# Seven quarter products for the second layer of the leading expert's first two blocks, with their gates made beside the last attention chunks and the row squares cleared by ScalarE

## The chip, the cores and the metric

The kernel runs on one core of one Trainium2 chip. The metric is the device time of one launch in microseconds; the median of three runs of the kernel before is 391.99 us (391.74 to 392.34).

## What is computed

A gated linear attention over 4 x 768 tokens and 8 heads of 48 dimensions gives rows of 384 features. Each of the 3,072 rows then goes to one of 8 experts by its cosine similarity, and the expert's two-layer network is scaled by the routing probability. Cut to what matters:

```python
state = alpha[:, :, t, :, None] * state + np.einsum('bhd,bhe->bhde', k[:, :, t], v[:, :, t])
y[:, :, t] = np.einsum('bhd,bhde->bhe', q[:, :, t], state)
...
logits = xn @ en.T / tau                      # xn, en: rows over their norms
expert_idx = np.argmax(logits, axis=1)
probs = np.exp(logits - logits.max(-1, keepdims=True)); probs /= probs.sum(-1, keepdims=True) + 1e-09
gate_w = probs[np.arange(N), expert_idx]
h = np.maximum(x[mask] @ w1[e], 0.0)          # 384 -> 1024
out[mask] = gate_w[mask, None] * (h @ w2[e])  # 1024 -> 384
```

## The kernel before

**The attention part** takes the tokens in 24 chunks of 128 rows. The loop over `s` is a software pipeline: in step `s` TensorE turns chunk `s`, VectorE runs two scans over it (`r` in `decays`, `a` in `decay_queries`), GpSimd multiplies the queries with `a` (`qs`), TensorE makes the scores of chunk `s - 1` (`sc`, masked by VectorE into `sm`), mixes chunk `s - 2` (`mix_states`, `mix_chunk`) and makes the output rows and router logits of chunk `s - 3` (`rows`). VectorE chooses experts by groups of chunks (`choose`, `place`), and GpSimd scatters each chunk's rows with their logits and token number to the DRAM buffer `xs`, sorted by expert (`to_rows`).

**The leading expert.** After 16 chunks some expert is sure to have 256 rows. It is found on VectorE (`first_expert`), and once chunk 15 is scattered, `fetch_early` has SyncE load its first two blocks of 128 rows into `exg` (the tile `xg_s[2]`). TensorE turns them (`turn_early`) and does their first layer in eight pieces beside the last three steps (`first_layer_early`, relu by ScalarE into `ehT`). After the last chunk VectorE counts the rows of each expert (`counts`, which ends with `pads` and `used_i`). GpSimd scatters blank rows behind each expert's rows (eight scatters of `blank` to `pads`) and clears the two tiles `xq` (two memsets); SyncE fetches the blocks of the experts in turn.

**The expert part** runs the experts in the order of turns, the leading one as number 0. Before `run(0)` come the gates of the two early blocks (`gates`: maximum, differences, row squares and root, exponential, sum, reciprocal, on VectorE and ScalarE) and their second layer, plain: `second_layer` multiplies eight tiles of 384 columns a block. Between the two blocks TensorE turns the rest of expert 0 (`prepare`), and VectorE forms the 16 sums of quarter weights for run 1's first layer (`mix_first_weights(1)`, 256 columns each). `run(0)` does the remaining block of expert 0 in the plain way, while TensorE turns run 1's four blocks through two PSUM tiles (`pxg`, `ps_x`) that VectorE copies out (`turn`, L919). Runs 1 to 7 use Strassen-like forms: 28 half-width products for the first layer of three blocks (`first_layer_blocks`) and seven quarter products for the second layer of two blocks (`second_layer_pair`). Those need four weight sums `w2_m` (`mix_weights`: 768 columns each, by VectorE for run 1, by GpSimd for the others) and four sums `hT_m` of the hidden rows (`mix_hidden`).

**What sets the order.** Each engine works through its own queue in a fixed order. The Tile scheduler sets that order by priorities and its own estimate of time; `tc.issue_after(x)` (`in_turn`, `behind`, `turn_of`, `by_dve`, `by_act`) keeps an instruction behind `x`. Waits between engines are semaphores at single instructions. In VectorE's queue the loads of the early rows are not waited for before the gates; on TensorE `turn_early` waits for them.

Of the kernel before, what the change touches and what calls it, by code (L numbers as in the profile page):

```python
# [29 lines left out]
def kernel(  # L30
# [16 lines left out]
    P = 128  # L47
# [63 lines left out]
    ehT = consts.tile([P, FT, EARLY * P], FP32)  # L111
    NXG = 3
# [113 lines left out]
    with ExitStack() as c1:  # L226
# [79 lines left out]
        def prepare_logits():  # L306

            nc.vector.reciprocal(rtau, rtau)
            e2 = work.tile([E, DM], FP32, name="e2", bufs=1)
            en = work.tile([E, 1], FP32, name="en", bufs=1)  # L310
            nc.scalar.activation(e2, emb, AF.Square, accum_out=en)
# [35 lines left out]
        def choose(g):  # L347
# [18 lines left out]
            for s in range(s0, s1):  # L366
                eng = nc.vector if {S0 - 1, NS - 1, NS - 2} & set(range(s0, s1)) else nc.gpsimd
                eng.tensor_tensor(before[:, s + 1], before[:, s], chosen[:, s], ALU.add)
# [52 lines left out]
        def counts(n):  # L421
# [20 lines left out]
            nc.vector.scalar_tensor_tensor(  # L442
# [12 lines left out]
            return nc.vector.tensor_copy(used_i, used[0:1])  # L455
# [180 lines left out]
        def mix_chunk(s):  # L636
# [4 lines left out]
            for hh in range(2):  # L641
# [7 lines left out]
                nc.scalar.copy(yT[hh].rearrange("p q t -> p (q t)"), pyx[hh][:, 0:YX])  # L649
# [46 lines left out]
        def first_layer_early(f0, f1):  # L696
            for f in range(f0, f1):
# [6 lines left out]
                nc.scalar.activation(ehT[:, f], ph, AF.Relu)  # L704


# [35 lines left out]
        for s in range(NS + 3):  # L742
# [33 lines left out]
            if NS <= s < NS + 2:  # L776
                with in_turn():
                    first_layer_early(2 * (s - NS), 2 * (s - NS) + 1)
# [16 lines left out]
            if NS <= s < NS + 2:  # L795
                with in_turn():
                    rows(s - 2)
# [31 lines left out]
            if s == NS:  # L829
                with tc.issue_after(st[NS - 1]["masked"].ins):  # L830
                    nc.gpsimd.memset(w1_s[1][:, 0, 0:1], 0.0)
                weights(1)
            for r in rows_of(s):
                g = group_of[r]
                if r == GROUPS[g][1] - 1:
                    with tc.issue_after(st[min(s, NS) - 1]["dve"].ins):
                        choose(g)
                    with behind(s) if s < NS else ExitStack():
                        nc.gpsimd.tensor_copy(x_g[g][:, :, TK], toks[:, slice(*GROUPS[g])])
            if s > NS:  # L840
                with in_turn():
                    first_layer_early(2 * (s - NS) + 2, 2 * (s - NS) + 4)
        with tc.issue_after(st[NS - 1]["dve"].ins):
            routed = [counts(n)]


    with ExitStack() as c3:
        qp = c3.enter_context(tc.tile_pool(name="qp", bufs=1, reuse_waits="tile"))
        xq_s.extend(qp.tile([P, NROW // SQ, DA], FP32, name=f"xq{i}") for i in range(NXQ))
# [10 lines left out]
        yp = c3.enter_context(tc.tile_pool(name="yp", bufs=3, reuse_waits="tile"))  # L860
# [8 lines left out]
        w2_m = wp.tile([P, 4, FT // 2, DM // 2], FP32, name="w2_m")  # L869
        hT_m = xp.tile([P, 4, FT // 2, P], FP32, name="hT_m")  # L870

# [6 lines left out]


# [344 lines left out]
        def second_layer_pair(w2_t, hT, gate, col):  # L1224
# [6 lines left out]
            a, b, d = (bank(j)[:, 0:m] for j in (0, 1, 3))  # L1231
# [28 lines left out]
            gated(y1[:, m:DM], a, g1, u[:, 2])  # L1260
            product(d, s4, b22, False, True)
# [3 lines left out]
            done_pair[:] = pe[0], by_act(nc.scalar.mul, y1[:, 0:m], a, g1)  # L1265
# [34 lines left out]
        def run(i):  # L1300
# [132 lines left out]
        egt = xp.tile([P, EARLY], FP32, name="egt")  # L1433
        esx = xp.tile([P, EARLY], I32, name="esx")
        known = gates(exg[:, 0:EARLY], egt[:, 0:EARLY], esx[:, 0:EARLY], EARLY)
# [9 lines left out]
        with turn_of([known]):  # L1445
# [38 lines left out]
```

## Time and profile before

| | us |
|---|---|
| median of three runs | 391.99 (391.74 to 392.34) |
| the profiled execution | 391.01 |
| its span, first to last instruction | 389.3 |
| TensorE busy in it | 379.9 |
| VectorE busy | 283.9 |
| GpSimd busy | 261.7 |
| ScalarE busy | 194.3 |

The profile is of one execution. A row of the timeline gives start, duration, engine, line, operation, written tile and read tiles, shape and count; in square brackets stand the idle time before it and what ended it. `PE` is TensorE, `DVE` VectorE, `ACT` ScalarE, `POOL` GpSimd, `SPq` the queue of SyncE. A matmul of this type has two records. Several instructions of one kind in a row are one row, whose duration runs from the first start to the last end; in a stream the next row starts before that end.

### The profile page before, as it was taken

How to read it: one execution, taken by the hardware profiler on the slowest of the kernel's cores; microseconds unless marked ns; L12 is line 12 of the kernel's file. 1: busy time of each engine (PE TensorE's matmuls, PEld its weight loads, DVE VectorE, ACT ScalarE, POOL GpSimd, SP SyncE). 2: the span in 40 equal slices, each digit the busy share in tenths (PEclk: the TensorE clock that was granted, in tenths of full speed). 3: DMA queues.
4: the chain of work that ended last, by engine and by line, in shares of the span. 5: the costliest groups of instructions: out<-in, count | busy, mean ns of one | idle time of the engine just before them, and what ended most of it. 6: DMA issues, size and time to landing. Idle time of an engine off the chain costs nothing. (4 is left out here: it accounts for less than half of the span.)

```text
span 389.3 us, 12413 instructions
## 1 busy us (share of the span) xinstructions
PE 379.9 (98%) x4596; PEld 338.3 (87%) x4596; DVE 283.9 (73%) x687; ACT 194.3 (50%) x492; POOL 261.7 (67%) x342
## 2 busy tenths in 40 slices
PE   6999999999999999999999999999999999999994
PEld 5889899999999877779989889789979979979974
DVE  7898989889999637992973984963874596795630
ACT  3555565554556544573653734823651492472620
POOL 5365577788776548744829959929957997977201
PEclk9999999999999999999999999999999999999999
DMA  9999999999999996794947768245604810100101
GB/s 138 162 166 166 156 182 197 190 182 198 187 218 174 285 370 231 214 355 97 356 109 285 212 197 287 46 154 182 180 19 175 296 28 18 43 2 17 40 19 46
DMA packets 131181, 64.05 MB, mean 165 GB/s; under 512 B 113319, under 2 KB 127920, under 8 KB 130344
## 3 DMA queue, kind: packets, MB, share of 16 engines
q1 hardware_dynamic: 127008, 52.92, 58.2%
q0 software_dynamic: 3728, 10.16, 7.3%
q8 instruction: 43, 0.70, 0.8%
q14 instruction: 26, 0.21, 0.2%
q10 hardware_dynamic: 376, 0.05, 0.1%
HBM read 53.85 MB, written 11.45 MB: 168 GB/s over the span
## 5 line engine op out<-in xcount | busy, mean ns | idle before, releaser
L1035 DVE TENSOR_TENSOR hT<-hT,pq 128x384 f32<-128x384 f32 x84 | 44.0, 549 | 35.9 <-PE pq L1143 28.4
L889 POOL DMA_INDIRECT out_dram<-y,sx x25 | 29.7, 1188 | 54.3 <-ACTq L1381 20.3
L538 POOL TENSOR_TENSOR qs<-qc,a 128x512 f32<-128x512 f32 x24 | 30.8, 1283 | 30.0 <-DVE a L534 20.8
L1143 PE MATMUL pq<-xT_m,w_m 128*128 128x192 f32 x252 | 44.4, 326 | 0.0
L1017 PE MATMUL pyo<-w,hT 128*128 128x384 f32 x128 | 42.6, 486 | 0.0
L1143 PEld LDWEIGHTS pq<-xT_m,w_m 128*128 128x128 f32 x252 | 41.4, 190 | 0.2
L1017 PEld LDWEIGHTS pyo<-w,hT 128*128 128x128 f32 x128 | 24.1, 190 | 14.8
L1040 ACT ACTIVATE hT<-hT 128x384 f32<-128x384 f32 x56 | 26.3, 515 | 15.2 <-DVE hT L1035 14.6
L1097 POOL TENSOR_TENSOR w_m<-w,w_m 128x256 f32<-128x256 f32 x42 | 31.1, 753 | 2.0 <-PE pq L1143 0.6
L1055 POOL TENSOR_TENSOR w_m<-w 128x768 f32<-128x768 f32 x12 | 23.9, 1991 | 11.7 <-PE pq L1240 11.7
L335 POOL DMA_INDIRECT xs<-x,dest x24 | 24.3, 1013 | 10.4 <-DVE dest L392 5.0
L534 DVE TENSOR_TENSOR_SCAN a<-pa,ini 128x512 f32<-128x512 f32 x24 | 29.3, 1222 | 1.0
L505 DVE TENSOR_TENSOR_SCAN r<-pa,inr 128x511 f32<-128x511 f32 x24 | 29.3, 1220 | 0.7
L1097 POOL TENSOR_TENSOR w_m<-w 128x256 f32<-128x256 f32 x36 | 28.2, 800 | 2.2 <-DVE xT_m L1113 1.4
L1240 PE MATMUL pq<-w_m,hT_m 128*128 128x192 f32 x168 | 28.6, 327 | 0.0
L1240 PEld LDWEIGHTS pq<-w_m,hT_m 128*128 128x128 f32 x168 | 27.4, 190 | 0.5 <-issue 0.5
L217 PE MATMUL pyx<-sm,vt 128*64 128x128 f32 x384 | 26.3, 279 | 0.0
L217 PE MATMUL sc<-qs,kr 64*64 64x128 f32 x768 | 25.6, 271 | 0.0
L217 PEld LDWEIGHTS pyx<-sm,vt 128*64 128x64 f32 x384 | 20.5, 136 | 4.1 <-issue 3.6
L1040 ACT ACTIVATE hT<-pq 128x384 f32<-128x384 f32 x28 | 13.7, 490 | 17.8 <-PE pq L1143 17.8
L1247 DVE SCALAR_TENSOR_TENSOR y<-pq,gt,u 128x192 f32<-128x192 f32 x21 | 8.6, 416 | 18.8 <-PE pq L1240 12.8
L1240 PEld LDWEIGHTS pq<-w,hT 128*128 128x128 f32 x112 | 18.4, 190 | 4.5 <-issue 2.6
(231 smaller groups left out, 986.2 us busy)
## 6 DMA issues: line engine op xcount, KB each, us to landing
w<-in_moe_w_dram SPq DMA_DIRECT2D x12, 1536.0 KB
w<-in_moe_w_dram SPq DMA_DIRECT2D x16, 384.0 KB
at<-in_alpha_dram SPq DMA_DIRECT2D x24, 192.0 KB
kt<-in_k_dram SPq DMA_DIRECT2D x24, 192.0 KB
qt<-in_q_dram SPq DMA_DIRECT2D x24, 192.0 KB
vt<-in_v_dram SPq DMA_DIRECT2D x24, 192.0 KB
xg<-xs SPq DMA_DIRECT2D x22, 196.5 KB
xq<-xs SPq DMA_DIRECT2D x72, 48.0 KB
```

The source lines that it names most:

```text
L217: last["pe"] = nc.tensor.matmul(*args, **kwargs)
L335: ins = nc.gpsimd.indirect_dma_start(out=xs, out_offset=bass.IndirectOffsetOnAxis(ap=rows, axis=0), in_=x, in_offset=None, bounds_check=E ...
L505: nc.vector.tensor_tensor_scan(r[:, L - 2 :: -1], pa[:, L - 1 : 0 : -1], inr[:, L - 2 :: -1], 1.0, ALU.mult, ALU.add,)
L534: d["a_scan"] = by_dve = nc.vector.tensor_tensor_scan(a, pa, ini, 0.0, ALU.mult, ALU.add)
L538: by_pool = nc.gpsimd.tensor_tensor(qs.rearrange("p n t -> p (n t)"), d["qc"], a, ALU.mult)
L889: ins = nc.gpsimd.indirect_dma_start(out=out, out_offset=bass.IndirectOffsetOnAxis(ap=col, axis=0), in_=y, in_offset=None, bounds_check=N - 1,
L1017: pe[:] = [nc.tensor.matmul(py, lhsT=hT[:, f], rhs=w2_t[:, f], start=(f == 0), stop=(f == FT - 1),)]
L1035: dve[:] = [call(*args, **kwargs)]
L1040: act[:] = [call(*args, **kwargs)]
L1097: by(w[to], w[x], w[y], op)
L1143: pe[:] = [nc.tensor.matmul(to[:, f], lhsT=w[left][:, f * P : (f + 1) * P], rhs=x[right], start=start and f == 0, stop=stop, skip_group_ch ...
L1240: pe[:] = [nc.tensor.matmul(to, lhsT=left[:, f], rhs=right[:, f], start=start and f == 0, stop=stop and f == n - 1, skip_group_check=True,)]
```

## The change

- The second layer of the two early blocks becomes one call of `second_layer_pair` on `ehT`: seven quarter products, with the four weight sums `w2_m` and the four sums `hT_m` made by VectorE ahead of it. The call takes a function `middle` (`prepare_lead`): the transposes of expert 0's rest and its gates, after the fifth product. In that call other PSUM banks are used, and the last gated copy is VectorE's.
- The gates of the early blocks (`early_gates`) are a generator whose pieces are issued beside steps 24 and 25. Its first four instructions read `exg` on VectorE; squares, root and exponential are ScalarE's.
- The weight sums `w2_m` of run 1 go to GpSimd, as those of the later runs.
- The two tiles `xq` are cleared by four copies of `blank` on ScalarE and not by two memsets on GpSimd.
- `w2_m`, `hT_m` and the tiles `y` come from pools opened earlier, and the square of the expert embeddings uses a part of a `vt` tile.

VectorE's queue in step 22, from the key product `kr` on (`sm` is the mask product of the scores, `state` the carried state, `x` the router logits; `xg_94` is the tile `exg`). Before:

```order
L512 TENSOR_TENSOR kr<-pk,r_133 128x512
L530 RECIPROCAL ini_135<-r_133 128x4
L534 SCALAR_TENSOR_TENSOR a<-pa,ini_135 128x512
L605 TENSOR_TENSOR sm_2865<-sc_2867,causal 128x512
L588 TENSOR_TENSOR state<-pd,dec 128x256
L353 TENSOR_REDUCE x<-lg 128x4x8
L358 TENSOR_REDUCE top<-x 128x4
```

Now:

```order
L517 TENSOR_TENSOR kr<-pk,r_135 128x512
L535 RECIPROCAL ini_137<-r_135 128x4
L539 SCALAR_TENSOR_TENSOR a<-pa,ini_137 128x512
L726 TENSOR_REDUCE top_e<-xg_94 128x2
L727 TENSOR_SCALAR none_e<-xg_94 128x2
L732 TENSOR_TENSOR sh_e<-xg_94,top_e 128x16
L728 SCALAR_TENSOR_TENSOR esx<-xg_94,none_e 128x2
L610 TENSOR_TENSOR sm_2870<-sc_2872,causal 128x512
L593 TENSOR_TENSOR state<-pd,dec 128x256
L357 TENSOR_REDUCE x<-lg 128x4x8
L362 TENSOR_REDUCE top<-x 128x4
```

Four instructions on the early rows stand between the scan `a` and `sm`.

GpSimd's queue after the last chunk, from the scatters of blank rows to the first sums of quarter weights for run 2. Before:

```order
L335 DMA xs<-blank,pads 25024x393 x2
L855 MEMSET xq_3351 128x1344
L855 MEMSET xq_3352 128x1344
L335 DMA xs<-blank,pads 25024x393 x6
L889 DMA out_dram<-y,esx 3072x384 x2
L1097 TENSOR_TENSOR w_m<-w_2_3412 128x256 x2
L889 DMA out_dram<-y,sx_3423 3072x384
```

Now, with the weight sums of run 1 (768 columns):

```order
L339 DMA xs<-x,dest 25024x393 x8
L339 DMA xs<-blank,pads 25024x393 x8
L1110 TENSOR_TENSOR w_m<-w_1_98 128x768
L1110 TENSOR_TENSOR w_m<-w_1_98,w_m 128x768
L1110 TENSOR_TENSOR w_m<-w_1_98 128x768
L944 DMA out_dram<-y,esx 3072x384
L1110 TENSOR_TENSOR w_m<-w_1_98,w_m 128x768
L944 DMA out_dram<-y,esx 3072x384
L1152 TENSOR_TENSOR w_m<-w_2_3431 128x256 x2
L944 DMA out_dram<-y,sx_3440 3072x384
```

The two memsets are gone, and four sums stand behind the eighth scatter, two output scatters among them.

VectorE's queue ahead of the copies of run 1's transposed rows (`w_m` of 256 columns are the sums for run 1's first layer, `gt` the gates of expert 0). Before:

```order
L1097 TENSOR_TENSOR w_m<-w_1_94,w_m 128x256
L910 TENSOR_SCALAR gt_3420<-gt_3420 128x2
L1097 TENSOR_TENSOR w_m<-w_1_94,w_m 128x256
L910 RECIPROCAL gt_3420<-gt_3420 128x2
L1097 TENSOR_TENSOR w_m<-w_1_94 128x256
L1097 TENSOR_TENSOR w_m<-w_m 128x256
L1097 TENSOR_TENSOR w_m<-w_1_94,w_m 128x256
L1097 TENSOR_TENSOR w_m<-w_m 128x256
L919 COPY xT_3415<-pxg 128x3x128 x3
L1113 TENSOR_TENSOR xT_m<-xT_3415 128x192 x2
```

Now:

```order
L1323 TENSOR_SCALAR y<-pq_3456,egt 128x192
L1152 TENSOR_TENSOR w_m<-w_1_96,w_m 128x256 x2
L1152 TENSOR_TENSOR w_m<-w_1_96 128x256
L965 TENSOR_REDUCE gt_3437<-gsh 128x2
L1152 TENSOR_TENSOR w_m<-w_m 128x256
L965 TENSOR_SCALAR gt_3437<-gt_3437 128x2
L1152 TENSOR_TENSOR w_m<-w_1_96,w_m 128x256
L965 RECIPROCAL gt_3437<-gt_3437 128x2
L1152 TENSOR_TENSOR w_m<-w_m 128x256
L974 COPY xT_3434<-pxg 128x3x128 x2
L1168 TENSOR_TENSOR xT_m<-xT_3434 128x192
```

The last sums stand ahead of the copies in both, with the last gated copy of the early blocks among them now.

The diff, cut to its core:

```diff
-        for x in xq_s:
-            with tc.issue_after(routed[-1].ins):
-                nc.gpsimd.memset(x, 0.0)
...
+        def early_gates():
+
+            shp = [P, EARLY, E]
+            l = exg[:, 0:EARLY, LG : LG + E]
+            token = exg[:, 0:EARLY, TK : TK + 1]
+            v = nc.vector
+            v.tensor_reduce(top_e.unsqueeze(2), l, axis=AX.X, op=ALU.max)
+            v.tensor_scalar(none_e, token, 1.0, float(FAR), ALU.is_lt, ALU.mult)
+            v.scalar_tensor_tensor(
+                out=esx.unsqueeze(2), in0=token, scalar=-1.0, in1=none_e,
+                op0=ALU.add, op1=ALU.add,
+            )
+            v.tensor_tensor(sh_e, l, bc(top_e, shp, 2), ALU.subtract)
+            for t in range(EARLY):
+                nc.scalar.activation(
+                    x2_e, exg[:, t, 0:DM].rearrange("p (h d) -> p h d", d=D), AF.Square,
+                    accum_out=sq_e[:, t],
+                )
+                yield
...
+            if s == NS:
+                gating = early_gates()
+                with tc.issue_after(turned_up.ins):
+                    next(gating)
...
                 with in_turn():
-                    mix_chunk(s - 2)
+                    cols_done = mix_chunk(s - 2)
+                if s == NS:
+                    with tc.issue_after(cols_done.ins):
+                        next(gating)
+                        scaled = next(gating)
...
-        def second_layer_pair(w2_t, hT, gate, col):
+        def second_layer_pair(w2_t, hT, gate, col, middle=None):
...
             gated(y1[:, m:DM], a, g1, u[:, 2])
+            if middle:
+                middle()
             product(d, s4, b22, False, True)
...
-                if i == 1:
-                    mix_weights(w2_t, lambda *args: by_dve(nc.vector.tensor_tensor, *args))
-                else:
-                    mix_weights(w2_t, nc.gpsimd.tensor_tensor)
+                mix_weights(w2_t, nc.gpsimd.tensor_tensor)
...
-        for t in range(EARLY):
-            if t == EARLY - 1:
-                for b in range(len(slots(0))):
-                    prepare(0, b)
-                ready = [prepare_gates(0)]
-            second_layer(
-                w2_s[0], ehT[:, :, t * P : (t + 1) * P], egt[:, t : t + 1], esx[:, t : t + 1]
-            )
...
+        def clear(i, h):
+            x = xq_s[i][:, h * NQR : (h + 1) * NQR]
+            return nc.scalar.copy(x, bc(blank[:, 0:DA], [P, NQR, DA], 1))
...
+        with turn_of([scaled]):
+            nc.vector.tensor_tensor(t1, b12, b11, ALU.subtract)
+        with turn_of([group_done]):
+            nc.vector.tensor_tensor(t3, b22, b12, ALU.subtract)
+        dve[:] = routed[0:2]
+        for to, x, y, op in (
+            (t2, b22, t1, ALU.subtract), (s1, a21, a22, ALU.add), (s2, s1, a11, ALU.subtract),
+            (s3, a11, a21, ALU.subtract), (s4, a12, s2, ALU.subtract),
+            (t4, b21, t2, ALU.subtract),
+        ):
+            by_dve(nc.vector.tensor_tensor, to, x, y, op)
+        mixed = list(dve)
+        second_layer_pair(w2_s[0], ehT, egt, esx, prepare_lead)
...
+        with turn_of(mixed):
             mix_first_weights(1, nc.vector.tensor_tensor)
```

## Rows read from the trace of the kernel before

**Rows 1.** the page, part 1: busy us, share of span, instructions
```profile
PE 379.9 (98%) x4596; PEld 338.3 (87%) x4596; DVE 283.9 (73%) x687; ACT 194.3 (50%) x492; POOL 261.7 (67%) x342
```

**Rows 2.** timeline of TensorE, 148 to 172 us: start us, us, engine, line, operation
```profile
150.75 6.61 PE L1017 MATMUL pyo<-w,ehT 128*128 128x384 f32 x20
...
157.20 0.96 PE L917 MATMUL pxg<-ident,xg 128*128 128x128 f32 x6
...
161.87 1.50 PE L1003 MATMUL pq<-xT,w 128*128 128x128 f32 x12
...
166.57 0.50 PE L917 MATMUL pxg<-ident,xg 128*128 128x128 f32 x3
```

**Rows 3.** timeline of VectorE, 118 to 134 us, the last attention chunks
```profile
124.15 1.23 DVE L534 TENSOR_TENSOR_SCAN a<-pa,ini 128x512 f32<-128x512 f32 x1
125.29 0.67 DVE L605 TENSOR_TENSOR sm<-sc,causal 128x512 f32<-128x512 f32 x1
...
129.72 1.22 DVE L534 TENSOR_TENSOR_SCAN a<-pa,ini 128x512 f32<-128x512 f32 x1
...
133.57 0.69 DVE L605 TENSOR_TENSOR sm<-sc,causal 128x512 f32<-128x512 f32 x1 [1.71 <-PE sc L217]
```

**Rows 4.** timelines of GpSimd and of TensorE around the last scores
```profile
131.09 1.27 POOL L538 TENSOR_TENSOR qs<-qc,a 128x512 f32<-128x512 f32 x1 [0.16 <-DVE a L534]
...
132.41 1.10 PE L217 MATMUL sc<-qs,kr 64*64 64x128 f32 x32
```

**Rows 5.** timeline of TensorE, two quarter products of a later expert
```profile
232.19 1.46 PE L1240 MATMUL pq<-w,hT_m 128*128 128x192 f32 x8
233.49 1.46 PE L1240 MATMUL pq<-w_m,hT 128*128 128x192 f32 x8
```

**Rows 6.** timeline of VectorE, 128 to 172 us, from the end of the counts
```profile
150.81 0.95 DVE L1035 TENSOR_TENSOR w_m<-w 128x768 f32<-128x768 f32 x1
...
157.53 0.17 DVE L910 TENSOR_REDUCE gtop<-xg 128x2 f32<-128x16 f32 x1 [0.21 <-DMA xg<-xs]
...
159.77 1.09 DVE L1097 TENSOR_TENSOR w_m<-w 128x256 f32<-128x256 f32 x3
...
165.85 1.01 DVE L919 COPY xT<-pxg 128x384 f32<-128x384 f32 x2
```

**Rows 7.** timeline of ScalarE, a relu of the first layer for the early rows
```profile
140.72 0.38 ACT L704 ACTIVATE ehT<-phe 128x256 f32<-128x256 f32 x1 [1.20 <-PE phe L217]
```

**Rows 8.** timeline of the queue of SyncE, the fetch of the early rows
```profile
125.66 0.39 SPq L207 DMA_DIRECT2D xg<-xs  x1
```

**Rows 9.** DMA packets of 126 to 128.5 us, all queues
```profile
DMA packets 285, 0.42 MB, mean 166 GB/s; under 512 B 16, under 2 KB 285, under 8 KB 285
```

**Rows 10.** timeline of GpSimd, 128 to 176 us: scatters of blank rows and memsets
```profile
150.99 1.61 POOL L335 DMA_INDIRECT xs<-blank,pads  x1 [0.50 <-DVE none L910]
...
154.48 2.40 POOL L855 MEMSET xq<- 128x1344 f32 x2
157.05 0.97 POOL L335 DMA_INDIRECT xs<-blank,pads  x1 [0.17 <-issue]
...
163.69 1.29 POOL L335 DMA_INDIRECT xs<-blank,pads  x1 [0.30 <-issue]
```

**Rows 11.** timeline of GpSimd, a weight sum of 768 columns of a later expert
```profile
203.50 1.80 POOL L1055 TENSOR_TENSOR w_m<-w 128x768 f32<-128x768 f32 x1 [3.55 <-PE pq L1240]
```

**Rows 12.** timelines of VectorE and GpSimd, 169.3 to 169.9 us, side by side
```profile
169.33 0.35 DVE L1113 TENSOR_TENSOR xT_m<-xT,xT_m 128x192 f32<-128x192 f32 x1
169.59 0.88 DVE L1118 TENSOR_TENSOR xT_m<-xT 128x192 f32<-128x192 f32 x1
...
169.49 0.77 POOL L1097 TENSOR_TENSOR w_m<-w 128x256 f32<-128x256 f32 x1 [1.44 <-DVE xT_m L1113]
```

**Rows 13.** stretches at the end: us, busy by engine, PEclk, DMA share, GB/s
```profile
384.00:385.00 1.00, 0.35 (x3) 0.05 (x1) 0.00 (x0) 0.42 (x1) 0.75 (x1) 1.00 0.08 25
...
387.00:388.00 1.00, 0.00 (x0) 0.00 (x0) 0.00 (x0) 0.00 (x0) 0.00 (x0) 0.75 0.23 79
```

More of the change, by code (lines that the diff above doesn't have):

```diff
@@ L111 @@
     ehT = consts.tile([P, FT, EARLY * P], FP32)
+    egt = consts.tile([P, EARLY], FP32)
+    esx = consts.tile([P, EARLY], I32)
     NXG = 3
@@ L367, in choose @@
                 eng = nc.vector if {S0 - 1, NS - 1, NS - 2} & set(range(s0, s1)) else nc.gpsimd
-                eng.tensor_tensor(before[:, s + 1], before[:, s], chosen[:, s], ALU.add)
+                done = eng.tensor_tensor(before[:, s + 1], before[:, s], chosen[:, s], ALU.add)
+            return done
         def place(g, total=False):
@@ L648, in mix_chunk @@
                     )
-                nc.scalar.copy(yT[hh].rearrange("p q t -> p (q t)"), pyx[hh][:, 0:YX])
+                done = nc.scalar.copy(yT[hh].rearrange("p q t -> p (q t)"), pyx[hh][:, 0:YX])
+            return done
         def rows(s):
@@ L703, in first_layer_early @@
                     )
-                nc.scalar.activation(ehT[:, f], ph, AF.Relu)
+                done = nc.scalar.activation(ehT[:, f], ph, AF.Relu)
+            return done
+        x2_e = at_s[0][:, :, 0:D]
+        sq_e = work.tile([P, EARLY, 1], FP32, name="sq_e", bufs=1)
+        sh_e = work.tile([P, EARLY, E], FP32, name="sh_e", bufs=1)
+        top_e = work.tile([P, EARLY], FP32, name="top_e", bufs=1)
+        none_e = work.tile([P, EARLY, 1], FP32, name="none_e", bufs=1)
+        def early_gates():
[11 more added lines that the diff above has]
+            for t in range(EARLY):
+                nc.scalar.activation(
+                    x2_e, exg[:, t, 0:DM].rearrange("p (h d) -> p h d", d=D), AF.Square,
+                    accum_out=sq_e[:, t],
+                )
+                yield
+            nc.scalar.activation(sq_e, sq_e, AF.Sqrt)
+            v.tensor_scalar(sq_e, sq_e, 1e-6, None, ALU.add)
+            v.reciprocal(sq_e, sq_e)
+            yield v.tensor_tensor(sh_e, sh_e, sq_e.to_broadcast(shp), ALU.mult)
+            nc.scalar.activation(sh_e, sh_e, AF.Exp)
+            yield
+            v.tensor_reduce(egt.unsqueeze(2), sh_e, axis=AX.X, op=ALU.add)
+            v.tensor_scalar(egt, egt, 1e-9, None, ALU.add)
+            yield v.reciprocal(egt, egt)
         def warm(n):
@@ L796 @@
                 with in_turn():
-                    rows(s - 2)
+                    copied = rows(s - 2)
+                if s == NS:
+                    with tc.issue_after(copied.ins):
+                        next(gating)
             if s == 1:
@@ L836 @@
                     with tc.issue_after(st[min(s, NS) - 1]["dve"].ins):
-                        choose(g)
+                        group_done = choose(g)
+                    if s == NS:
+                        with tc.issue_after(group_done.ins):
+                            early_gated = next(gating)
                     with behind(s) if s < NS else ExitStack():
@@ L877 @@
         sx_s = [xp.tile([P, NC + 1], I32, name=f"sx{i}") for i in range(NG)]
+        for j in range(4):
+            ps_q.tile([P, 512], FP32, name=f"pq{j}")
         taken = []
@@ L1230, in second_layer_pair @@
             (a11, a12), (_, a22) = (hidden(hT, t) for t in range(2))
-            a, b, d = (bank(j)[:, 0:m] for j in (0, 1, 3))
+            a, b, d = (bank(j)[:, 0:m] for j in ((3, 1, 2) if middle else (0, 1, 3)))
             y0 = yp.tile([P, DM], FP32, name="y")
```

55 lines of the change are left out of this document (37 added, 18 removed).

## The prediction

> **What bounds the kernel now.** The busy share of the engines comes first: TensorE works nearly all of the span and the other four have room [rows 1]. So a change counts if it shortens TensorE's own work or makes TensorE wait. The second view is TensorE's row of work around the leading expert's first two blocks [rows 2]: the second layer starts at 150.75, six transposes stand in it from 157.20, and the expert's remaining block starts at 161.87, with no idle time noted between; that is 11.12 us. The third view is VectorE in the last chunks of the attention part [rows 3]. From 124.15 to 131.85 one instruction follows the other, and the first idle time is the 1.71 us before 133.57. In that stretch VectorE leads TensorE by nothing: the scan at 129.72 frees GpSimd's product, that ends at 132.36, and the scores on TensorE start at 132.41 [rows 3, 4]. What VectorE loses before 131 us TensorE loses too.
>
> **The products (the gain).** Two plain second layers are 32 matmul records of 384 columns, and with six transposes (0.80 us) they fill the 11.12 us [rows 2]. Seven quarter products are 56 records of 192 columns. A product of 8 records takes 1.30 us from start to start in the experts that already work so (232.19 to 233.49) [rows 5]. So 7 x 1.30 = 9.10, and with the transposes 9.90: **1.2 us less**.
>
> What must be there in time: the third product needs the row sum s2 and the weight sum t2. VectorE reaches t2 where it now starts w_m at 150.81 [rows 6], then makes s1 and s2 of 512 columns, which cost no more than the 0.95 of that 768-column sum: s2 is there by 153.65 at the latest, while two products end at 153.35. That is 0 to 0.3 us; I take 0, as the sums are a third shorter. t1 and t3 lie in idle stretches of VectorE. The gates' ScalarE parts (two squares, root, table load, exponential) and two of the four clears come ahead of relus of the first layer, which today wait 1.20 us for TensorE [rows 7]; TensorE takes a relu's result only through one of three PSUM buffers, so I cost them at nothing, and at 0.5 if a buffer runs out. The third clear stands right before the first gated copy. By the 0.38 of 256 columns [rows 7] its 672 take at most 1.0, so that copy is done near 152.9, before the third product. The square of the expert embeddings only changes its buffer, at the start: nothing.
>
> **First wait: the early gates on VectorE.** The changed order puts four small instructions on the early rows (top_e, none_e, sh_e, esx) right behind the scan of 124.15 and in front of the mask product sm of 125.29. The scan ends at 125.38, and the first of the four reads the rows that SyncE only begins to fetch at 125.66 [rows 8]. The change doesn't move that fetch: it follows the scatter of chunk 15's tokens. Its 393 KB are 256 packets of 1.5 KB: with a few packets of the weights they have moved by 128.5, when the 16 packets under 512 B that close a transfer stand in the count too [rows 9]. So VectorE stands from 125.38 to about 128.45, then does the four (0.17 each [rows 6], overlapping: some 0.45), and sm starts near 128.9, not at 125.29: **3.6 us late**. Behind it on the same queue are sm, the state, the routing of a group, the next scan, kr and the scan of 129.72; GpSimd's product and the scores wait for that, and no cover is left [rows 3, 4]. The 1.71 us of idle time before 133.57 don't help: there VectorE waits for TensorE, which is late itself. Everything after it (pads, fetches, gates) hangs on this chain and moves along. Bounds: 3.1 if the rows have landed half a microsecond before that window ends, 4.0 if the closing packets count half a microsecond late.
>
> **Second wait: four weight sums that move to GpSimd.** Run 1's second-layer sums (768 columns each) leave VectorE and join GpSimd's queue behind eight scatters of blank rows. The two memsets leave GpSimd. Today the first two scatters run from 150.99 to 154.48 and the other six from 157.05 to 164.98 [rows 10]; without the memsets the eight end near 154.8 + 7.93 = 162.7, and there three sums of 1.8 us each [rows 11] start back to back. VectorE meanwhile has 16 sums of 256 columns for run 1's first layer (0.34 each in a row, from the 1.09 of three with its tail) and then the copies of transposed rows that start at 165.85 today [rows 6]. With four of the 16 done before the rows land (157.53) and the evictions much alike, they would start at 164.5. So at 162.7 VectorE still has about five of its sums to do, beside GpSimd's three.
>
> What that costs is in the trace at one place: GpSimd's sum of 0.77 us from 169.49 stands beside VectorE's xT_m of 169.59, which takes 0.88 where the same shape takes 0.35 just before; it ends 0.2 after GpSimd's [rows 12]. A VectorE sum of two SBUF inputs waits for the GpSimd sum to end. The Trainium skill says so too, and it speaks against this change: GPSIMD Engine Reference, section 1 Specifications, has GpSimd's SBUF interfaces shared with VectorE, in contention where VectorE reads two SBUF inputs.
>
> One VectorE sum between two of GpSimd, then: three get through while GpSimd works (162.7 to some 169.1), the other two after it, and the copies start near 169.7. The third group of run 1's transposes on TensorE (166.57 today [rows 2], 165.35 with the 1.2 saved) needs a PSUM buffer that the first copy frees, at 170.2. **4.8 us of wait on TensorE.** It would be 0 if GpSimd began after 164.5, about 1 with one sum left, 3 with two, 5.5 with GpSimd's sums delayed too. I take 4.8, since the estimate of five sums has to be wrong by three to halve it. The later scatters on GpSimd move back some 4 us; their y buffers have a third copy, so I cost that at nothing.
>
> **Sum.** -1.2 + 3.6 + 4.8 = +7.2. The profiled execution took 391.01 (span 389.3 and 1.7 around it), below all three timed runs; on it the sum is 398.2, on the median of the runs, 391.99, it is **399.2 us**, which I forecast.
>
> **Rivals.**
> *The clock falls in the second wait.* TensorE's granted clock is 1.00 while it works and is down to half (1.2 GHz) in the course of the microsecond from 387, after matmuls ended in that from 384 [rows 13]: some three microseconds of nothing. The second wait is longer; the first is no longer than that, and a chunk's products fall into it. What follows at the low level costs its own length again: 1.7 if it is what remains of the first layer (12 records and three transposes [rows 2]), 6.8 if it goes on through the second layer. I take 1.7: 400.9. TensorE: Matmul & The Clock Gate, Part 1, in the Trainium skill has the same two levels and lets the lower one follow idle time; the trace agrees at 387.
> *GpSimd and VectorE miss each other.* If the scatters end after 164.5 or VectorE is 1.5 us further, only the first wait is left: 391.99 - 1.2 + 3.6 = 394.4. For it: both estimates add up many small steps. Against it: the six scatters would have to be a quarter slower than today.
> *Not slower: a waiting VectorE instruction is passed by later ones.* If sm starts although top_e waits, and the copies although a sum waits, both prices are nothing and the saving stays: 390.8. It decides at whether sm starts before 128. For it: neighbouring VectorE records overlap by some 0.1 us. Against it: the idle time before 133.57 has ready work behind it that doesn't move up.
> *The first wait is hidden, the second not* (a fetch some 3 us faster): 395.6.
>
> **How the numbers follow.** Forecast 399.2: 0.42. Clock: 0.28. Only the first wait: 0.16. Passed: 0.07. Only the second: 0.05. The last 0.02 I give to no change. The range takes in the first three: from 394.4 (with the lower bound of the wait, 393.9) to 402.0 (400.9 with the upper bounds of the waits, 0.4 and 0.7 more). A measurement of this kernel tells about 0.2% (0.8 us) from no change: faster 0.07, within 0.2% 0.02, slower 0.91.
>
> **What would show it.** In the changed kernel's profile: idle time of about 3 us on VectorE before top_e, put down to the fetch of xg; scores on TensorE near 136 instead of 132.4; the seven products and transposes in 9.9 us; VectorE's sums of 256 columns drawn out to 2 us beside GpSimd's of 768; idle time on TensorE before a transpose of pxg in run 0, put down to VectorE's copy. The prediction is wrong if sm follows the scan at once, or if GpSimd's first sum begins when VectorE's are done.

## The result and the profile after

The changed kernel takes 397.14 us (median of six runs, 395.71 to 400.15), the kernel before beside it 392.16 us (391.74 to 393.04): a ratio of 1.0137, 95% interval 1.0106 to 1.0168. The profiled execution of the changed kernel took 395.71 us with a span of 394.0 us, 4.7 us more than the span of 389.3 before. TensorE is as long busy as before (379.7 us; [rows 1] has 379.9) in a longer span, so the loss is waiting. In two groups of runs below, those of `e10`, `e9` and `e5` and of the repetitions, the kernel before took 402.6 and 402.8 us and not 392, so of these only ratios within the group, and rows that show a mechanism, are used. The page, part 1:

```profile
PE 379.7 (96%) x4620; PEld 342.0 (87%) x4620; DVE 292.1 (74%) x693; ACT 197.8 (50%) x499; POOL 269.4 (68%) x344
```

TensorE's own view of its waits after 110 us (us in total, times, longest) names four; before the change it names none there:

```profile
PE pxg L972 <- DVE xT L974: 3.0, 1, 3.0
PE px L219 <- DVE state L593: 1.6, 1, 1.6
PE pxe L222 <- DVE a L539: 0.7, 1, 0.7
PE pyo L1339 <- DVE y L1076: 0.5, 1, 0.5
```

**The first wait.** VectorE's timeline, the same stretch as [rows 3], and under it the fetch of the early rows on SyncE's queue and the last scores on TensorE, as in [rows 8] and [rows 4]:

```profile
123.42 1.22 DVE L539 TENSOR_TENSOR_SCAN a<-pa,ini 128x512 f32<-128x512 f32 x1
126.83 0.17 DVE L726 TENSOR_REDUCE top_e<-xg 128x2 f32<-128x16 f32 x1 [2.19 <-DMA xg<-xs]
...
127.19 0.68 DVE L610 TENSOR_TENSOR sm<-sc,causal 128x512 f32<-128x512 f32 x1
...
131.70 1.22 DVE L539 TENSOR_TENSOR_SCAN a<-pa,ini 128x512 f32<-128x512 f32 x1
...
135.53 0.69 DVE L610 TENSOR_TENSOR sm<-sc,causal 128x512 f32<-128x512 f32 x1 [1.71 <-PE sc L219]
```

```profile
123.78 0.39 SPq L209 DMA_DIRECT2D xg<-xs  x1
```

```profile
134.38 1.10 PE L219 MATMUL sc<-qs,kr 64*64 64x128 f32 x32
```

VectorE stands for 2.19 us for the early rows. From the scan to the last scores it was 8.26 us before (124.15 to 132.41) and is 10.96 now (123.42 to 134.38): 2.7 us lost. The 1.71 us before the last `sm` stand unchanged: that idle time hides nothing.

**The products.** TensorE's timeline from the second layer of the early blocks on, as in [rows 2]:

```profile
152.71 2.76 PE L1295 MATMUL pq<-w,ehT 128*128 128x192 f32 x16
155.31 4.07 PE L1295 MATMUL pq<-w_m,hT_m 128*128 128x192 f32 x24
159.21 0.95 PE L972 MATMUL pxg<-ident,xg 128*128 128x128 f32 x6
159.99 1.47 PE L1295 MATMUL pq<-w,hT_m 128*128 128x192 f32 x8
161.29 1.46 PE L1295 MATMUL pq<-w_m,ehT 128*128 128x192 f32 x8
162.59 1.50 PE L1058 MATMUL pq<-xT,w 128*128 128x128 f32 x12
...
170.47 0.61 PE L972 MATMUL pxg<-ident,xg 128*128 128x128 f32 x3 [3.00 <-DVE xT L974]
...
180.95 1.62 PE L1339 MATMUL pyo<-xT,w 128*64 128x64 f32 x48 [0.51 <-DVE y L1076]
```

From 152.71 to 162.59 it is 9.88 us, 1.24 less than the 11.12 of before, without a gap. The sums, gates and clears beside them cost TensorE nothing.

**The second wait** is the 3.00 us before 170.47. GpSimd's and VectorE's timelines in that stretch, as in [rows 10] and [rows 6]:

```profile
164.37 1.43 POOL L339 DMA_INDIRECT xs<-blank,pads  x1 [0.30 <-issue]
165.81 1.83 POOL L1110 TENSOR_TENSOR w_m<-w 128x768 f32<-128x768 f32 x1
167.72 1.94 POOL L1110 TENSOR_TENSOR w_m<-w,w_m 128x768 f32<-128x768 f32 x1
169.63 1.99 POOL L1110 TENSOR_TENSOR w_m<-w 128x768 f32<-128x768 f32 x1
```

```profile
165.29 2.39 DVE L965 TENSOR_SCALAR gt<-gt 128x2 f32<-128x2 f32 x1
167.59 0.41 DVE L1152 TENSOR_TENSOR w_m<-w,w_m 128x256 f32<-128x256 f32 x1
167.93 0.15 DVE L965 RECIPROCAL gt<-gt 128x2 f32<-128x2 f32 x1
168.00 1.94 DVE L1152 TENSOR_TENSOR w_m<-w_m 128x256 f32<-128x256 f32 x1
169.87 1.01 DVE L974 COPY xT<-pxg 128x384 f32<-128x384 f32 x2
```

The two engines take turns: a gate of two columns takes 2.39 us and a sum of 256 columns 1.94 (0.41 elsewhere), each ending within 0.3 us of the end of one of GpSimd's sums (167.64 and 169.66), and in the turn between them one sum of VectorE takes 0.41. The copies from PSUM at 169.87 aren't held, though GpSimd's third sum runs until 171.6.

**What nobody had counted.** The chunks' transfers are faster in the changed kernel. Stretches of the start (us, busy by engine, PEclk, DMA share, GB/s), before and after:

```profile
0.00:35.00 35.00, 31.32 (x536) 27.31 (x538) 29.41 (x71) 17.10 (x41) 18.44 (x53) 1.00 1.12 158
```

```profile
0.00:35.00 35.00, 32.18 (x556) 28.33 (x556) 30.77 (x71) 17.79 (x43) 18.85 (x54) 1.00 0.96 189
```

In the start TensorE waited 2.0 us in all for the chunks' loads before, and waits for none of them now. The scan of [rows 3] starts 0.73 us earlier (123.42 against 124.15).

### The profile page after: what moved, and what is told of

Its sections match the earlier page's. It is cut to its first block, busy times and chain, and to the rows that moved or that the text cites. A ratio compares the mean times of both kernels' runs of the same rounds, so it can differ in the third digit from the quotient of the medians.

```text
span 394.0 us, 12483 instructions
## 1 busy us (share of the span) xinstructions
PE 379.7 (96%) x4620; PEld 342.0 (87%) x4620; DVE 292.1 (74%) x693; ACT 197.8 (50%) x499; POOL 269.4 (68%) x344
## 3 DMA queue, kind: packets, MB, share of 16 engines
q1 hardware_dynamic: 127008, 52.92, 51.9%
## 5 line engine op out<-in xcount | busy, mean ns | idle before, releaser
L1110 POOL TENSOR_TENSOR w_m<-w 128x768 f32<-128x768 f32 x14 | 27.8, 1986 | 11.5 <-PE pq L1295 11.4
L1295 PE MATMUL pq<-w_m,hT_m 128*128 128x192 f32 x192 | 32.7, 327 | 0.0
L339 POOL DMA_INDIRECT xs<-x,dest x24 | 25.2, 1049 | 9.9 <-DVE dest L397 5.0
L1295 PEld LDWEIGHTS pq<-w_m,hT_m 128*128 128x128 f32 x192 | 31.3, 190 | 0.5 <-issue 0.5
L1110 POOL TENSOR_TENSOR w_m<-w,w_m 128x768 f32<-128x768 f32 x14 | 25.7, 1833 | 0.7
L685 ACT COPY lg<-pyx 128x32 f32<-128x32 f32 x24 | 4.4, 185 | 37.1 <-PE px L219 37.1
```

The costliest lines, as they stand in the source:

```text
L1110: by(to, x, y, ALU.subtract)
L1295: pe[:] = [nc.tensor.matmul(to, lhsT=left[:, f], rhs=right[:, f], start=start and f == 0, stop=stop and f == n - 1, skip_group_check=True,)]
```

## The experiments

### The gates behind the last sums

```diff
-                with tc.issue_after(turned_up.ins):
+                with tc.issue_after(turned_up.ins), tc.issue_after(st[NS - 1]["dve"].ins):
                     next(gating)
```

> The four early-gate operations are put behind the last step's sums in VectorE's stream instead of between its scan and its sums; all else is as in the changed kernel. Theory (the early rows' fetch holds VectorE, and TensorE's last scores with it): the wait of 2.2 us ahead of the row maximum goes, the last scores start 2.7 us earlier, and the time falls by about 2.7 us, from 397.1 to 394.4; the second wait of 3.0 us before the transposes of run 1's rows stays, and with it whatever scatter its executions have. Rival (the wait only replaces one that comes anyway, on a transfer that ends at a fixed time): under 0.7 us is gained.

394.63 us (12 runs, 392.38 to 396.68), ratio 1.0057 (1.0034 to 1.0079): 2.5 us less than the changed kernel's 397.14. TensorE's only wait of more than 0.3 us after the start is the one for the copies, still 3.0. The last scores on TensorE:

```profile
130.94 1.10 PE L219 MATMUL sc<-qs,kr 64*64 64x128 f32 x32
```

From the scan (122.69) to them it is 8.25 us, as the 8.26 of before. So the first wait is the four instructions' place in VectorE's queue and nothing else. That the times differ by nearly its 2.7 us is in part chance: in the profiles the start is another 0.73 us earlier, the wait at the half block is gone, and the clock, below, takes 1.7 us back.

The runs spread by 4.3 us, and time goes roughly with the mean granted clock: the two at 1.000 took 392.38 and 392.80, the three at 0.988 to 0.990 took 395.54 to 396.68, though one at 0.997 took 395.93. The profiled one (0.993, 393.44) shows where. TensorE's timeline behind the 3.0 us, and stretches of the same time:

```profile
167.18 0.61 PE L972 MATMUL pxg<-ident,xg 128*128 128x128 f32 x3 [3.01 <-DVE xT L974]
167.63 2.37 PE L1058 MATMUL pq<-xT,w 128*128 128x128 f32 x12
169.78 0.85 PE L972 MATMUL pxg<-ident,xg 128*128 128x128 f32 x3
170.42 5.85 PE L1072 MATMUL pyo<-w,hT 128*128 128x384 f32 x16
```

```profile
166.00:168.00 2.00, 0.82 (x7) 0.83 (x8) 1.97 (x4) 0.00 (x0) 2.00 (x2) 1.00 1.02 386
168.00:170.00 2.00, 2.00 (x13) 2.00 (x12) 2.00 (x4) 0.28 (x1) 1.81 (x3) 0.52 1.07 388
170.00:172.00 2.00, 2.00 (x7) 1.37 (x7) 2.00 (x3) 1.91 (x7) 1.83 (x2) 0.63 1.12 345
```

After 3.0 us without a matmul the granted clock is 0.52, so the lower level of 1.2 GHz, for some 3 us. The same groups took 1.50, 0.50 and 5.33 at full clock: 0.87 + 0.35 + 0.52 = 1.7 us. In the profiled execution of the changed kernel the same wait of 3.0 us left the clock at 1.00.

### The weight sums later: a wait that moves

```diff
-                mix_weights(w2_t, nc.gpsimd.tensor_tensor)
+                with turn_of(done_pair[-1:] if i == 1 else []):
+                    mix_weights(w2_t, nc.gpsimd.tensor_tensor)
```

> Run 1's four weight sums on GpSimd are held behind the scatter of the leading expert's finished blocks, so they no longer run beside VectorE's sums; all else is as in the changed kernel. Theory (VectorE's reads of two SBUF inputs stand still while a GpSimd sum of 768 columns runs): the 2.39 and 1.94 us operations on VectorE go back to under 0.9, the 3.0 us in which TensorE waits for the copies of run 1's rows goes to at most 0.5, the time falls by about 3.0 us to 394.1, and the executions agree better, since the wait in which the clock can fall is gone. Rival (VectorE is late there because of its own work, gates moved into that stretch): the TensorE wait stays over 2 us and the time within 1 us of 397.1. Second rival (the sums, now late, hold run 1's second layer): a new TensorE wait after 185 us takes back what the first gives.

400.87 us (399.64 to 401.19), ratio 1.0207 (1.0184 to 1.0230): slower than the changed kernel by 3.7 us. The operations of 2.39 and 1.94 us take 0.16 and 0.40 again and the wait of 3.0 us is gone, as the theory said; but a wait of 6.4 us now stands before 213.59, so the second rival was right that a new wait takes back the gain, and it takes more. The first wait is still there, and in this profile the granted clock fell behind it, where TensorE had waited 1.7 us: it is 0.50 in the microsecond from 129.

```profile
129.00:130.00 1.00, 1.00 (x28) 1.00 (x24) 1.00 (x2) 1.00 (x5) 0.00 (x0) 0.50 0.95 278
```

With the gates moved as well:

> Both moves at once: early gates behind the last sums, run 1's weight sums behind the scatter. Theory (two waits, in series and independent): what is left of the change is the seven products, 1.2 us less than eight, and a half-block wait of 0.5 us: 391.0 to 391.5 against 392.2 before the change, a ratio of about 0.997 to before. Rival (the fetch's wait, once lifted, moves to the products' start, where the gates are wanted): about 393.5, with a wait on the gates ahead of the product's sums. Rival (a slower clock behind any idle stretch of TensorE explains most of the loss): no single wait explains it and both edits together give more than the sum of their waits, 390 or less.

397.53 us (396.92 to 399.58), ratio 1.0134 (1.0109 to 1.0160), where 391.0 to 391.5 was expected. Neither of the two waits is there; the one of 6.4 us stands in run 1's second layer. Timelines of VectorE, GpSimd and TensorE:

```profile
203.12 4.35 DVE L1173 TENSOR_TENSOR xT_m<-xT 128x192 f32<-128x192 f32 x2
207.39 2.01 DVE L1160 SCALAR_TENSOR_TENSOR xT_m<-xT_m 128x192 f32<-128x192 f32 x1
```

```profile
203.55 1.83 POOL L1110 TENSOR_TENSOR w_m<-w 128x768 f32<-128x768 f32 x1
205.46 1.80 POOL L1110 TENSOR_TENSOR w_m<-w,w_m 128x768 f32<-128x768 f32 x1
207.22 1.97 POOL L1110 TENSOR_TENSOR w_m<-w 128x768 f32<-128x768 f32 x1
```

```profile
211.01 2.90 PE L1295 MATMUL pq<-w_m,hT 128*128 128x192 f32 x8 [6.43 <-DVE y L1302]
```

Run 1's sums pushed GpSimd's quarter sums for run 2 back; these held VectorE until 202, so its row sums (two in 4.35 us, 0.35 each elsewhere) met the 768-column sums of run 2, and the gated copy behind them released TensorE's bank late. So the late sums hold run 1's second layer only by this detour. In the changed kernel VectorE has done its row sums at 207.8 and that GpSimd sum starts at 208.24. The mean clock is 0.983 to 0.991 in all 15 runs of this kernel, the one before and the next, which have this wait in their profiles; here the product at 211.01, eight records, took 2.90 us instead of 1.46, at a granted clock of 0.50.

The clears, put back to two GpSimd memsets:

```diff
+        for x in xq_s:
+            with tc.issue_after(routed[-1].ins):
+                nc.gpsimd.memset(x, 0.0)
...
-        with turn_of([early_up]):
-            clear(0, 0)
```

> The same as both moves, but the tiles of the row squares are cleared by two GpSimd memsets, as before the change, not by four ScalarE copies. Theory (a GpSimd memset holds VectorE's instructions with two SBUF inputs, as the 2.35 us row of before shows, beside the evictions' stretch which has slack): 0 to 0.5 us slower than both moves alone, since the held instructions are copies for which TensorE does not wait until later. Rival (the clears were what the products' evictions wait for): over 1 us slower than both moves alone.

398.03 us (397.50 to 398.67), ratio 1.0139 (1.0114 to 1.0165), with the same wait of 6.4: no difference to 397.53 that these runs can tell, though the 6.4 us behind the clears could hide a small one. The row of 2.35 us on which the expectation rests is an instruction with one input; beside the memsets of this run (2.41 us from 152.66) a sum of two SBUF inputs took 0.95 us as elsewhere, so the theory's hold did not come about.

### The weight sums in GpSimd's gap, in thirds, and earlier

In the first, the sums are issued behind the first two quarter sums for run 2 (with the gates moved); in the second, each is cut in three, in the changed kernel as it is; in the third, the last two blank scatters are held behind run 0's block.

```diff
-                    mix_first_weights(i + 1, nc.gpsimd.tensor_tensor)
+                    sums = []
+                    mix_first_weights(
+                        i + 1, lambda *args: sums.append(nc.gpsimd.tensor_tensor(*args))
+                    )
+                    if i == 1:
+                        with turn_of(sums[1:2]):
+                            mix_weights(w2_t, nc.gpsimd.tensor_tensor)
```

```diff
+        def by_thirds(to, x, y, op):
+            n = to.shape[2] // 3
+            for k in range(3):
+                nc.gpsimd.tensor_tensor(*(t[:, :, k * n : k * n + n] for t in (to, x, y)), op)
...
-                mix_weights(w2_t, nc.gpsimd.tensor_tensor)
+                mix_weights(w2_t, by_thirds if i == 1 else nc.gpsimd.tensor_tensor)
```

```diff
-                to_rows(pads[:, i + 2 : i + 3], blank)
+                with turn_of(done_pair[-1:] if i >= 4 else []):
+                    to_rows(pads[:, i + 2 : i + 3], blank)
```

> Early gates behind the last sums, as in the run with the gates later, and run 1's four weight sums on GpSimd behind the first two quarter sums for run 2, so after the copies of run 1's rows and ahead of the half block's scatter: GpSimd stands idle there for 2.7 and 5.8 us, and VectorE has little with two SBUF inputs to do. Theory (what the sums collide with sets the price, not that they are on GpSimd): neither the 3.0 us wait at the copies nor the 6.4 us wait at run 2's row sums comes; the time is 390.8 to 391.5 and the runs lie within 1 us of each other at a clock as before the change. Rival (four more GpSimd sums of 1.8 us cannot be placed without a wait, the two stretches being too short): a wait of 2 us or more of TensorE after 170 us, 394 or more. Rival (the seven products lose what they save, in bank waits): 392.2 or more with no wait over 1 us.

> Run 1's four GpSimd sums of 768 columns are cut into three of 256 columns each, in the same place, in the changed kernel as it is (early gates still ahead of the last sums). Theory (a VectorE instruction with two SBUF inputs waits for the end of the GpSimd instruction that runs, and then gets its turn): held operations last 0.7 to 1.1 us and not 1.9 to 2.4, so the copies come earlier and TensorE waits 1 to 2 us and not 3.0; the time falls by 1 to 2.5 us to 394.6 to 396.1. Rival (the two engines share a rate, whatever the size of an instruction): the held stretch and the 3.0 us stay within 0.5 us, the time within 0.7 us of the changed kernel's 397.1.

> The scatters of the last two blank rows are held back behind run 0's block, so run 1's four GpSimd sums start about 2.7 us earlier, beside more of VectorE's quarter sums; nothing else is changed in the changed kernel. Theory (each of VectorE's remaining sums waits for one GpSimd sum; with the start 1.15 us earlier than it came the prediction had counted five sums left and a wait of 4.8): more sums are held, the wait ahead of the copies grows from 3.0 to 4.5 to 6 us, and the time by 1.5 us or more, to 398.6 or above. Rival (the start does not matter, GpSimd's sums end earlier by as much): wait 2.5 to 3.3 us, the time within 0.7 us of 397.1.

The medians were 407.98, 409.36 and 409.99 us where before took 402.57 (398.40 to 408.24). In all three ScalarE, VectorE or both stand still in the middle of the early blocks' products, with nothing of the core's own named as what ended it ("remote"). ScalarE's timeline in the first:

```profile
167.78 0.73 ACT L1095 ACTIVATE u<-pq,egt 128x192 f32<-128x192 f32 x2 [10.38 <-remote]
```

TensorE waited 7.9 us of this for ScalarE. That shifts all that follows, so `e5` tells nothing of the start of the sums: its GpSimd sums began 11.0 us after the products did (13.1 in the changed kernel), but within the products TensorE waited 4.1 us for ScalarE. The first two were run once more, with the changed kernel beside them:

> The kernel with the gates behind the last sums and run 1's sums in GpSimd's gap, once more: in its first runs the kernel before the change took 402.6 us too, and ScalarE stood still for 10.4 us ahead of a gated copy with nothing that the trace names in its way. Theory: without that stillness neither of the two waits is there, 390.8 to 391.5, ratio to before 0.996 to 0.998, and the runs lie within 1 us. Rival (the sums cannot be placed without a wait): a wait of 2 us or more after 170 us, 394 or more. Rival (ScalarE's stillness belongs to this order and not to those executions): it is there again, and the time is 397 or more where before takes 392.

> The changed kernel with run 1's four GpSimd sums cut into thirds, once more, for the same reason. In the first runs VectorE's operations beside the thirds took 0.70 to 0.95 us, where they had taken 1.94 and 2.39 beside the whole sums, and TensorE waited 0.7 us for the copies. Theory (VectorE waits for the end of one GpSimd instruction, whatever its length): the same held times, a wait of 0.5 to 1.5 us and not 3.0, and 394.6 to 396.1 us. Rival (a shared rate): the 3.0 us stay within 0.5 us, and the time within 0.7 us of the changed kernel.

> The changed kernel as it is, for more executions beside the kernel before and beside the two above. Theory: the two waits of 2.2 and 3.0 us stand in every execution; where the clock also falls in or behind the second wait the time is 2 to 4 us longer: 395.7 to 400.2 us, the longer ones at the lower clock, and the ratio to before is 1.011 to 1.017. Rival (the scatter is one of the chip and not of the clock): time and clock of the executions do not go together, and the kernel before scatters as much.

Before took 402.79 us; the three took 407.59, 408.84 and 411.34, ratios 1.0134 (1.0081 to 1.0188), 1.0185 (1.0135 to 1.0235) and 1.0227 (1.0169 to 1.0284). The same stillness is there in all three, and the scatter can't be put down to the clock: it is 0.980 to 0.984 in all six of the changed kernel. But the rows of VectorE beside GpSimd tell the mechanism apart. In the changed kernel of this group (GpSimd's whole sums of 1.82 us) two gates meet them; TensorE then waits for gated copies queued behind:

```profile
171.46 1.80 DVE L965 TENSOR_TENSOR gsh<-xg,gtop 128x16 f32<-128x16 f32 x1
...
176.65 2.43 DVE L965 TENSOR_TENSOR gsh<-gsh,gsq 128x16 f32<-128x16 f32 x1
```

```profile
175.99 0.94 PE L1058 MATMUL pq<-xT,w 128*128 128x128 f32 x6 [2.54 <-DVE y L1302]
...
179.81 2.93 PE L1058 MATMUL pq<-xT,w 128*128 128x128 f32 x12 [2.53 <-DVE y L1323]
```

With the sums in thirds the same two gates are held for a third of the time, and so is TensorE:

```profile
175.48 0.78 DVE L965 TENSOR_TENSOR gsh<-xg,gtop 128x16 f32<-128x16 f32 x1
...
178.65 0.74 DVE L965 TENSOR_TENSOR gsh<-gsh,gsq 128x16 f32<-128x16 f32 x1
```

```profile
180.11 1.60 PE L1058 MATMUL pq<-xT,w 128*128 128x128 f32 x12 [0.84 <-DVE y L1328]
...
184.06 0.62 PE L972 MATMUL pxg<-ident,xg 128*128 128x128 f32 x3 [0.67 <-DVE xT L974]
```

So an operation of VectorE of the kinds held here waits for the end of one GpSimd instruction, whatever its length, and gets the next turn; a shared rate would have left the waits as they were. With the whole sums in the gap, neither of the two waits is there, but three row sums are held for 1.96 or 1.97 us each, the eviction comes behind them, and TensorE waits 2.0 us at the half block, as the first rival of `e10` had it.

### Thirds in the gap

The gates moved, the sums in the gap, and in thirds: the diffs above, together.

> Gates behind the last sums, and run 1's sums in GpSimd's gap and cut into thirds of 256 columns, so that an operation of VectorE that meets one is held for 0.75 us at most and not for 1.9; with the whole sums in the gap the copies were free but the row sums and the eviction behind them were held, and TensorE waited 2.0 us at the half block. Theory: neither the first nor the second wait, the half block's wait under 0.7 us; 390.8 to 391.8 where before takes 392.2, and about 2.0 us less than the whole sums in the gap where the executions are slow ones (405.6 where before takes 402.7). Rival (twelve small sums cost GpSimd more than four and hold its scatters and the branch): a wait of over 1 us at the half block, 393 or more, or no better than the whole sums.

389.10 us (388.44 to 389.73) where before took 392.59 (391.43 to 393.94): a ratio of 0.9917 (0.9895 to 0.9940). This beats both kernels. TensorE is busy for all of 160 to 190 us, and the timelines of GpSimd and VectorE show why. The thirds stand beside the last row sums and the gates of run 1, each held for 0.9 us at most, and the eviction `y` is done at 173.7, while TensorE multiplies on:

```profile
168.64 2.43 POOL L1108 TENSOR_TENSOR w_m<-w 128x256 f32<-128x256 f32 x3
171.03 2.12 POOL L1108 TENSOR_TENSOR w_m<-w,w_m 128x256 f32<-128x256 f32 x3
```

```profile
171.13 0.66 DVE L965 TENSOR_SCALAR none<-xg 128x4 f32<-128x4 f32 x1
...
173.12 0.60 DVE L1076 TENSOR_SCALAR y<-pyo,gt 128x384 f32<-128x384 f32 x1
```

The runs lie within 1.3 us at clocks of 0.996 to 1.000. What lies below the expected 390.8 comes from the start, which no theory here had counted: in the profiled execution the scan of [rows 3] and the last scores (131.04) start 1.37 us before those of [rows 3, 4], and the products are 1.3 us shorter (149.37 to 159.20), together the 2.6 us by which its span of 386.7 is shorter. That the 1.37 us are the chunks' faster transfers is likely and not shown.

The kernel before, for a second profile:

> The kernel before the change, for a second profile of it, to see where its own 10 us go in the executions in which it takes 402.6 us and not 392.2. Theory (engines wait for their own instructions there, ScalarE and VectorE ahead of the products on the early rows, whichever kernel runs): ScalarE or VectorE stands still 2 to 8 us at 150 to 170 us with nothing in its way, as in the changed kernel. Rival (transfers are slower in all of the program): the attention's chunks are each later, and the loss is spread over 0 to 150 us. If the executions are at 392 us, the profile is as the first one and says nothing of this.

393.00 us, much as in the first profile, so what ScalarE and VectorE stood still for above, and where the kernel before lost 10 us there, stays open. It does say that the transfers are no accident of one profile: in the first 35 us they made 156 and 158 GB/s in the two profiles of before, and 181 to 189 in those of the changed kernel, `e1`, `e2`, `e3`, `e7` and `e12`. The scan of [rows 3] started at 124.15 and 125.74 in the former, and at 122.69 to 123.67 in the latter. So executions of one kernel differ by more than the 0.73 us above, and that number belongs to its two profiles alone.

## Why the prediction was right, and where its terms were off

It said 399.2 us, range 393.9 to 402.0, and slower with 0.91; it came to 397.14. Both waits it named are there, at the instructions it named, and `e1`, `e2` and `e12` show them as the cause. The sizes were too large: from profile to profile it is +4.7 (389.3 to 394.0) where the sum had +7.2. That the median still came within 2.1 us of the forecast is in part luck: three of its six runs are longer ones at a lower clock, for which the sum had no term. Term by term, between the profiles:

- **The products, -1.2:** -1.24, and the sums, gates and clears beside them for nothing, as costed.
- **The first wait, +3.6:** +2.7. The order of events was as told. Off was the step that put the fetch at 125.66, 1.51 us after the scan's start, with the sentence that the change doesn't move it. It is issued at 123.78, 0.36 us after the scan's start, and the rows are read at 126.83, 3.05 us later (estimated: 2.8). 3.6 - 1.15 + 0.25 = 2.7. The fetch waits for the rows of chunk 15 to land in DRAM. Before, that was 3.1 us after GpSimd's scatter was done (122.58), with chunk loads still issued around it; now it is 1.9 us (121.84), the last chunk load being issued at 113.3. The earlier fetch is no accident: it came 0.39 to 0.69 us after the scan's start in `e1`, `e2`, `e3`, `e7` and `e12`, and 2.20 in the second profile of before. That the chunk loads, done earlier, no longer delay the rows fits this and was not tried.
- **The second wait, +4.8:** +3.0. The turns between the engines were as told; the start was not. GpSimd's first sum came 13.1 us after the products' start (165.81 against 152.71) and not 11.95: the last six scatters took 9.65 us (156.15 to 165.80), and not the 7.93 of [rows 10]. The step that failed there is the one that took the memsets away and left the scatters' own time as it was: with the memsets ahead of them the six took 7.67 to 7.96 us in three profiles (both of before, and `e7`), without them 8.54 to 9.79 in five (the changed kernel, `e1`, `e2`, `e3`, `e12`); why is open. With the later start two operations of VectorE were held ahead of the copies, and not the three or more that five open sums made; the copies start 1.8 us earlier than told (169.87, or 167.9 counted from the old start of the products, against 169.7).
- **Not in the sum:** the earlier start, -0.73; and a wait of 0.5 at the half block, where the eviction comes behind held row sums (the prediction followed the held queue only as far as the copies). From start to start the two late waits cost a little more than their idle time: 162.59 to 172.59 is 3.28 more than the same work before (161.87 to 168.59), and the half block's first part 0.73 more (178.82 to 182.40 against 174.82 to 177.67). So -0.73 + 2.70 - 1.24 + 3.28 + 0.73 = 4.7, and TensorE resumes run 1's first layer that much later (185.10 against 180.37).
- **The rival of the clock** (400.9) was right in some executions and wrong in others, and its price of 1.7 us is the sum that the profile of `e1` shows, though 0.52 of it fell into the second layer. It left the first wait out; `e2` shows the clock at 0.50 behind that one too. The changed kernel's runs fit it: those at a mean clock of 0.992 to 1.000 took 395.7 to 396.6 us (the profiled one among them), those at 0.988 to 0.991 took 397.7 to 400.2; none of the latter was profiled, and 1.7 us is not all of that distance. TensorE: Matmul & The Clock Gate, Part 1, in the Trainium skill, lets the lower level follow idle time; the trace agrees at 168 us of `e1`, and shows with the changed kernel's own profile that 3.0 us of it don't always do it.
- **The other rivals:** `sm` doesn't pass the waiting `top_e` (127.19), GpSimd and VectorE don't miss each other, and both waits are there in one execution.

GPSIMD Engine Reference, section 1, in the Trainium skill, from which the prediction took support for the second wait, names VectorE instructions with two SBUF inputs and those in a 2-port mode. The trace agrees for the first kind: a sum of two SBUF inputs was held (1.94 us). The gate of 2.39 us, with one input of two columns, was held too; no run here shows whether it is of the second kind. The prediction had not counted it.

## What to carry over

An instruction that waits for a transfer costs its queue everything behind it, so ask what is queued there and not how small it is. Before an elementwise job goes to GpSimd, look up what VectorE does in that very stretch, and in those into which the rest of GpSimd's queue is pushed; in GpSimd's gap, and cut into pieces of 0.7 us, the four sums cost TensorE no wait here; whole, they cost 2.0 us in that gap, 3.0 where the change had put them, and 6.4 further back. What one wait costs is only known when it is taken away: taking away the second alone made the kernel slower by 3.7 us.

## What the runs showed of the hardware

- 3.0 us without a matmul halved TensorE's granted clock in one profile (`e1`, at a cost of 1.7 us) and left it at 1.00 in another (the changed kernel); the mean clocks of the runs say the same of executions of one kernel. Behind a wait of 1.7 us it fell to 0.50 in a third profile (`e2`), where the same wait left it at 1.00 in the changed kernel's (1.6 us). Behind the 6.4 us it was 0.50 (`e3`), and the mean clock was below 0.992 in all 15 runs.
- The same 127,008 packets and 52.92 MB on the queue of SyncE took 58.2% of the sixteen DMA engines' span before and 51.9% after the change. The change moved where tiles lie in SBUF; that this is the cause was not tried.
- A pair of GpSimd memsets held a VectorE instruction with one input of two columns to the end of the pair, and not a sum of two SBUF inputs. In the two profiles of before the former took 2.35 and 1.05 us instead of 0.16 and ended within 0.03 us of the pair (156.88 and 158.08); in the first a sum queued behind it came out with it. A sum of 768 columns that met the memsets by itself took 0.95 us (from 155.69 in the second profile, from 152.96 in `e7`), as elsewhere.
- In six profiles (`e10`, `e9` and `e5` and the repetitions) ScalarE or VectorE stood still in the middle of the early products, ScalarE for up to 10.4 us. What they waited for is open.
